# More filler products, a moved gate row, padded w_phi rows and a new nominal order in a fused attention and FFN kernel

## The chip, the cores and the metric

The kernel runs on one core of a Trainium2 chip. The time is the device time of one execution in microseconds (us). The times shown are those of 3 runs of the kernel before; beside them one execution was taken with the hardware profiler, and all rows of the profile come from that one.

## The reference, cut to what matters

The input is one sequence of 2048 tokens with 640 features. Two branches read the same x: a linear attention with 32 heads of 20 features, whose feature map is a softmax of plus and minus a small product with `w_phi`, and a gated FFN with 1728 hidden features. A gate for each token mixes the two.

```python
x = A_x                                                   # 1 x 2048 x 640
g = sigmoid((x * gate_w).sum(-1, keepdims=True))
qkv = (x @ wqkv).reshape(B, S, 3, 32, 20).transpose(2, 0, 3, 1, 4)
pq = einsum("bhsd,hdf->bhsf", q, w_phi)                   # the same for k
phi_q = concat([softmax(pq), softmax(-pq)])               # the same for k
kv = einsum("bhsf,bhsd->bhfd", phi_k, v);  z = phi_k.sum(s)
o = einsum(phi_q, kv) / (einsum(phi_q, z) + 1e-6)
a = o.transpose(...).reshape(B, S, 640) @ wo
b = (gelu(x @ w_gate) * (x @ w_up)) @ w_down              # hidden width 1728
out = g * a + (1 - g) * b
```

## The kernel before, in words

**Tiles.** Tokens are worked in 16 tiles of 128, and for the FFN in 4 blocks of 512. The hidden width is cut into 14 chunks per block (13 of 128 and one of 64 + 64). A chunk is five products for the gate weights `wg` and five for the up weights `wu` (line 647; 128x512 each, over five slices of the 640 features), then a GELU on ScalarE (line 661) and a product on VectorE (line 663). Keys, values and queries of a token tile are two halves of 320 columns, five products each (line 687). Evictions from PSUM go through one helper (line 593 on ScalarE, line 595 on VectorE).

**Folding.** `w_phi` is folded into the key and query weights. It is loaded into `w6`, 120 rows (six heads of 20) by six groups; GpSimd multiplies it with a mask into block-diagonal tiles `BD` (line 606); TensorE multiplies these with the transposed key weights `WkT` (line 621) and the results are evicted into `wK`. The fold has ten steps, for five slices of the features and two halves: groups 0 to 2, and groups 3 to 5. Later the same is done with `WT` for the queries.

**Start-up.** SyncE's queue issues nearly all loads: four token tiles `xtok`, the first 256 columns of `wg` and `wu`, the columns 256 to 640 of both, `w6`, the six transposed loads of `WkT`, the value weights `wV`, and then further FFN weights between transposed loads of x. `w6` takes two loads: one for the groups 0 to 4, one for the 40 rows that the last group has. TensorE first runs 18 useless products on a zeroed tile (`spin`, line 550), then transposes the token tiles 0 and 1 (line 559), runs 5 more useless products, and then the first products with `wg`. The gate vector is loaded as five rows of 128 (`grow`), turned by one tiny transpose on TensorE (line 573), and copied by VectorE (line 575) into a 641st column of `wV`, so that the value product also gives the gate's sums. Its load is issued from ScalarE's queue.

**The order.** The order isn't written by hand. Every operation is entered with a nominal priority, which comes from the table `TIMES` (start of a key group, its period, offsets of exponentials, chunks, folds, queries, attention and down projection) or from numbers beside the call in `startup`. A list scheduler on the host (`schedule`) then plays the program through: it has a duration for each operation, a byte count for each load (all loads share 300 KB per us, and a load counts as landed 1.6 us after its share), five engines and six PSUM banks. At each step it takes the engine that can start something first, and there the ready operation with the smallest priority. `HOLD` makes an operation that needs another ScalarE table look ready that much later. What comes out is the order in which each engine's instructions are emitted; each engine then runs its instructions strictly in that order and waits on semaphores where an operand isn't there.

Dependencies between operations go by cells of 32 bytes of a partition's memory (`CELL`): two operations that touch one cell, one of them writing, are ordered. A row of `w6` before is 20 values of 2 bytes, so 40 bytes a group; the groups 4 and 5 share a cell.

```python
        avail = {e: [] for e in self.obj}
...
            o = min((x for x in lst if from_(x) <= t + 1e-9), key=lambda x: (x.prio, x.idx))
...
            if o.dma:
                dma_free = max(dma_free, t + dur) + o.bytes / 300e3
                o.end = dma_free + 1.6
```

Of the kernel before, what the change touches and what calls it, by code (L numbers as in the profile page):

```python
# [7 lines left out]
P = 128  # L8
# [24 lines left out]
class _Prog:  # L33
# [73 lines left out]
    HOLD = 3.9  # L107
# [163 lines left out]
class _Kernel:  # L271
    S, D, H, F = 2048, 640, 32, 1728
    DH, KD, NT, NB, TB, BT = 20, 5, 16, 4, 4, 512
    NG, HPG = 6, 6
# [14 lines left out]
    def alloc(self):  # L289
# [47 lines left out]
        W = self.HPG * self.DH  # L337
        for name, shape in (("BD", [P, self.NG, W]), ("BM", [P, W]),
                            ("w6", [W, self.NG, self.DH]),
                            ("grow", [KD, P])):  # L340
            setattr(self, name, nc.alloc_sbuf_tensor_at(name, shape, BF, offset=b0))
            b0 += -(-int(np.prod(shape[1:])) * 2 // 64) * 64
# [51 lines left out]
    def at(self, T, fn, *args):  # L394
# [4 lines left out]
    TIMES = dict(wkp=-4.57, dfk=0.51, dfq=0.95, mask=-16.43, fold_k=12.18, t0=33.24, per=21.78, pair=3.13,  # L399
                 exp=3.84, ff=14.55, dff=2.71, fold_q=39.04, rest=-4.17, drest=-3.34, q=-38.61, dq=2.39,  # L400
                 qlate=13.99, q0pre=-21.12, q0exp=-8.41, q0post=1.5, at0=31.81, d0=53.28, q1pre=-18.21,
                 q1exp=2.34, q1post=25.29, f2=28.62, df=1.8, at1=10.48, d1=41.89, q2pre=4.15, q2exp=7.74,
                 q2post=13.74, f3=67.06, at2=21.14, d2=90.12, q3pre=-29.71, q3exp=6.32, q3post=17.94, at3=41.36,
                 d3=45.04)
# [41 lines left out]
    def startup(self):  # L446
        pr = self.pr
        D, KD = self.D, self.KD
        HPG, DH, NG = self.HPG, self.DH, self.NG
# [29 lines left out]
        dma("act", self.grow[:, :], self.gw_d.rearrange("(kt p) -> kt p", p=P), -30.0, 2000)  # L479
# [7 lines left out]
        def ffn_w(i, a, b):  # L487
            n = (b - a) * (1420 if b - a < 512 else 1070)
            dma("sp", self.wg[:, :, a:b], wg_r[:, :, a:b], i, n)
            dma("sp", self.wu[:, :, a:b], wu_r[:, :, a:b], i + 0.01, n)  # L490

        ffn_w(-7.5, 0, 256)
        ffn_w(-4.8, 256, 640)
# [15 lines left out]
        ffn_w(-4.4, 640, 1152)  # L509
# [6 lines left out]
        ffn_w(-4.19, 1152, self.FM)  # L516
# [37 lines left out]
        def tile(t, prio):  # L554
            bk = self.next_a()

            def tr(e):
# [443 lines left out]
```

## Time and profile before

| | |
|---|---|
| median of 3 runs | 293.33 us (291.94 to 294.5) |
| the profiled execution, its own time | 294.05 us |
| its span, first to last instruction | 291.5 us |
| TensorE matmul busy | 285.8 us (98%), 2123 products |
| VectorE busy | 210.7 us (72%) |
| ScalarE busy | 160.8 us (55%) |
| GpSimd busy | 11.6 us (4%) |
| moved by DMA | 24.24 MB, mean 83 GB/s |

The span leaves out what lies around the program, so it is shorter than the execution's own time by 2.55 us. Busy time of TensorE is modelled from the starts of pipelined products, so how fast it runs is read from the distance between starts. In rows of the timeline the columns are start (us), duration (us), engine, line, operation, output and input, shapes, count; in brackets stands the idle time ahead and what ended it. `SPq` is SyncE's queue: there the duration is that of the issue, not of the transfer.

### The profile page before, as it was taken

To read this page: it belongs to the slowest core of one execution; us is meant where nothing else is said; L and a number is where in the kernel's file an instruction comes from. 1 tells how busy PE (TensorE), PEld (TensorE's weight loads), DVE (VectorE), ACT (ScalarE), POOL (GpSimd) and SP (SyncE) were. 2 spreads that over 40 slices of the span, in tenths; PEclk is the share of its full clock that TensorE was granted. 3 is DMA by queue.
4 is the path that set the end of the run, shared out by engine and by line. 5 is a ranking of instruction groups with operands and counts; after the bars stand their busy time and mean duration, and the time that the engine had idled before them with its cause. 6 is when DMAs were issued, how large, how long until landed. Compare 5 with 4: busy or idle time off the path is not lost.

```text
span 291.5 us, 5260 instructions
## 1 busy us (share of the span) xinstructions
PE 285.8 (98%) x2123; PEld 180.8 (62%) x2123; DVE 210.7 (72%) x422; ACT 160.8 (55%) x274; POOL 11.6 (4%) x42
## 2 busy tenths in 40 slices
PE   7999999999999999999999999999999999999996
PEld 6747556567766566456577755655665444777775
DVE  1251799999959999999999999999895332623420
ACT  4318597998686599349917725952861223121121
POOL 8210002100000000000000000000000000000000
PEclk9999999999999999999999999999999999999999
DMA  7969956970000000000455364061313000782421
GB/s 207 199 173 329 176 116 115 297 168 0 2 0 2 0 0 3 0 3 7 92 74 117 93 147 66 9 144 47 72 45 74 0 0 2 135 130 74 92 67 45
DMA packets 61739, 24.24 MB, mean 83 GB/s; under 512 B 52803, under 2 KB 61123, under 8 KB 61715
## 3 DMA queue, kind: packets, MB, share of 16 engines
q1 hardware_dynamic: 60921, 20.83, 33.5%
q0 software_dynamic: 640, 3.03, 3.7%
q8 instruction: 16, 0.26, 0.4%
q14 instruction: 8, 0.07, 0.1%
q10 hardware_dynamic: 154, 0.04, 0.1%
HBM read 8.96 MB, written 2.62 MB: 40 GB/s over the span
## 4 chain that ended last, share of the span: by engine, by line
PE 94%; ACT 2%; DMA 1%; DVE 1%; issue 1%; SPq 0%
PE ps L647 39%; PE ps L687 21%; PE ps L935 21%; PE ps L944 7%; PE ps L756 2%; PE ps L892 2%; DMA wg<-in_B_w_gate_dram 1%; ACT E L803 1%; DVE wK L595 1%; PE ps L621 1%; ACT L803 0%; PE ps L559 0%; SPq L455 0%; ACT Sq L593 0%; ACT gel L661 0%
## 5 line engine op out<-in xcount | busy, mean ns | idle before, releaser
L935 PE MATMUL ps<-wd,hT 128*128 128x320 bf16 (+1 forms) x462 | 65.7, 295 | 0.0
L647 PE MATMUL ps<-xT,wg 128*128 128x512 bf16 (+1 forms) x270 | 63.1, 376 | 0.9 <-DMA wg<-in_B_w_gate_dram 0.8
L647 PE MATMUL ps<-xT,wu 128*128 128x512 bf16 (+1 forms) x270 | 62.7, 374 | 0.0
L661 ACT ACTIVATE gel<-ps 128x512 bf16<-128x512 f32 (+1 forms) x56 | 32.6, 597 | 54.0 <-PE ps L647 53.8
L663 DVE TENSOR_TENSOR hT<-ps,gel 128x512 bf16<-128x512 f32 (+1 forms) x56 | 38.5, 688 | 24.1 <-PE ps L647 23.1
L935 PEld LDWEIGHTS ps<-wd,hT 128*128 128x128 bf16 x462 | 43.5, 98 | 16.2
L821 DVE TENSOR_REDUCE dn<-E 128x132 f32<-128x2640 bf16 x16 | 46.3, 2898 | 4.8 <-ACT E L803 4.7
L950 ACT ACTIVATE osb<-ps,Gm 128x320 bf16<-128x320 f32 (+1 forms) x33 | 16.7, 516 | 52.3 <-PE ps L944 52.1
L647 PEld LDWEIGHTS ps<-xT,wg 128*128 128x128 bf16 x270 | 26.3, 99 | 27.5 <-DVE xT L595 1.4
L647 PEld LDWEIGHTS ps<-xT,wu 128*128 128x128 bf16 x270 | 26.3, 99 | 25.9
L803 ACT ACTIVATE E<-E 128x1320 bf16<-128x1320 bf16 x32 | 40.9, 1307 | 0.6 <-DVE E L796 0.5
L687 PE MATMUL ps<-wK,xT 128*128 128x320 bf16 x160 | 25.7, 299 | 0.7 <-DVE wK L595 0.7
L782 DVE TENSOR_TENSOR t<-t 128x132 bf16<-128x132 bf16 (+1 forms) x96 | 25.2, 262 | 1.0
L687 PE MATMUL ps<-wV,xT 128*128 128x321 bf16 (+1 forms) x160 | 25.7, 300 | 0.0
L687 PE MATMUL ps<-wQ,xT 128*128 128x320 bf16 x160 | 24.4, 299 | 0.2 <-ACT Sq L593 0.2
L687 PEld LDWEIGHTS ps<-wK,xT 128*128 128x128 bf16 x160 | 15.5, 98 | 8.1 <-DVE wK L595 0.8
L900 DVE SCALAR_TENSOR_TENSOR zt<-dn,ps 128x18 f32<-128x18 f32 (+1 forms) x32 | 5.4, 167 | 20.8 <-PE ps L892 20.8
L687 PEld LDWEIGHTS ps<-wQ,xT 128*128 128x128 bf16 x160 | 15.4, 98 | 7.2 <-ACT Sq L593 0.6
L687 PEld LDWEIGHTS ps<-wV,xT 128*128 128x128 bf16 x160 | 15.4, 98 | 7.1
L944 PE MATMUL ps<-wo,OT 128*128 128x320 bf16 (+1 forms) x125 | 19.4, 294 | 0.0
L842 DVE TENSOR_TENSOR E<-E,r 128x2640 bf16<-128x2640 bf16 (+1 forms) x16 | 18.8, 1177 | 0.0
L593 ACT ACTIVATE Sk<-ps 128x320 bf16<-128x320 f32 x32 | 13.9, 448 | 7.2 <-PE ps L687 6.9
(80 smaller groups left out, 254.3 us busy)
## 6 DMA issues: line engine op xcount, KB each, us to landing
out_dram<-osb SPq DMA_DIRECT2D x15, 160.0 KB, 1.8
wd<-in_B_w_down_dram POOLq DMA_DIRECT2D x1, 2080.0 KB, 11.8
wg<-in_B_w_gate_dram SPq DMA_DIRECT2D x2, 640.0 KB, 5.9
wu<-in_B_w_up_dram SPq DMA_DIRECT2D x2, 640.0 KB, 6.6
wV<-in_A_wqkv_dram SPq DMA_DIRECT2D x1, 800.0 KB, 4.7
wo<-in_A_wo_dram POOLq DMA_DIRECT2D x1, 800.0 KB, 12.8
xtok<-in_A_x_dram SPq DMA_DIRECT2D x4, 160.0 KB, 3.3
wg<-in_B_w_gate_dram SPq DMA_DIRECT2D x1, 480.0 KB, 5.7
```

The lines of the kernel that those rows point to most:

```text
L593: self.pr.op("act", lambda e: e.activation(dst, src(), AF.Copy), reads=[bk], writes=[dst], dur=_act(n), prio=prio)
L647: i = e.matmul(out, w[:, kt, :], x[:, kt, :], start=kt == 0, stop=kt == self.KD - 1)
L661: pr.op("act", lambda e: e.activation(g2, self.bank(pg)[r0, :], AF.Gelu_apprx_tanh), reads=[pg], writes=[gs], dur=_act(512), prio=prio, ta ...
L663: pr.op("dve", lambda e: e.tensor_tensor(h, self.bank(pu)[r1, :], g2, ALU.mult), reads=[gs, pu], writes=[h], dur=_dve(512, 1, True), prio= ...
L687: i = e.matmul(self.bank(bk, n), x[:, kt, :], w[:, kt, :], start=kt == 0, stop=kt == self.KD - 1)
L782: pr.op("dve", lambda e: e.tensor_tensor(o, a, b, op), reads=[a, b], writes=[o], dur=_dve(el, rate), prio=T + q)
L803: self.pr.op("act", lambda e, dj=dj: e.activation(dj, dj, AF.Exp), reads=[dj], writes=[dj], dur=_act(1320), prio=T + 0.01 * j, table="exp")
L821: pr.op("dve", lambda e: e.tensor_reduce(dn, d4, AX.X, ALU.add), reads=[d4], writes=[dn], dur=_dve(20 * H), prio=T)
L842: pr.op("dve", lambda e: e.tensor_tensor(dd, dd, m, ALU.mult), reads=[dd, r2], writes=[dd], dur=_dve(20 * H, 2), prio=T + 0.03)
L935: i = e.matmul(out, self.hT[:, hs, c, j * P:(j + 1) * P], self.wd[:, c, c0:c1], start=c == 0, stop=False)
L944: i = e.matmul(out, ot[:, k, :], self.wo[:, k, c0:c1], start=False, stop=k == self.KD - 1)
L950: pr.op("act", lambda e, dst=dst, bk=bk, n=n, gm=gm: e.activation(dst, self.bank(bk, n), AF.Copy, scale=gm), reads=[bk, gm], writes=[dst], ...
```

## The change

Five things are edited together.

- The useless products between the transposes of the token tiles 0 and 1 and the first `wg` products become twelve instead of five.
- The load of the gate row moves from ScalarE's queue to SyncE's, with a priority just behind the four token tiles. The tiny transpose of it gets priority 1.8 instead of 1.4, that is, behind the transposes of the token tiles 2 (1.6) and 3 (1.7).
- `w6` gets rows of 32 values (64 bytes) for each group, of which 20 are used; the loads and the masks address those 20.
- The scheduler's prices of transposed loads change: `WkT` and `WT` 220,000 bytes instead of 400,000 (1.31 us of issue instead of 1.3), x 180,000 instead of 380,000 (1.31 instead of 1.6).
- `HOLD` and the numbers of `TIMES` are replaced, so the order of the whole program is a new one.

The helper `ffn_w` gets more parameters; all calls still use SyncE's queue with the same pieces.

```diff
-    HOLD = 3.9
+    HOLD = 2.7
...
-                            ("w6", [W, self.NG, self.DH]),
+                            ("w6", [W, self.NG, 32]),
...
-    TIMES = dict(wkp=-4.57, dfk=0.51, dfq=0.95, mask=-16.43, fold_k=12.18, t0=33.24, per=21.78, pair=3.13,
-                 exp=3.84, ff=14.55, dff=2.71, fold_q=39.04, rest=-4.17, drest=-3.34, q=-38.61, dq=2.39,
-                 qlate=13.99, q0pre=-21.12, q0exp=-8.41, q0post=1.5, at0=31.81, d0=53.28, q1pre=-18.21,
-                 q1exp=2.34, q1post=25.29, f2=28.62, df=1.8, at1=10.48, d1=41.89, q2pre=4.15, q2exp=7.74,
-                 q2post=13.74, f3=67.06, at2=21.14, d2=90.12, q3pre=-29.71, q3exp=6.32, q3post=17.94, at3=41.36,
-                 d3=45.04)
+    TIMES = dict(wkp=-4.68, dfk=1.33, dfq=1.03, mask=4.05, fold_k=7.07, t0=40.19, per=21.68, pair=1.74,
+                 exp=12.53, ff=13.58, dff=2.78, fold_q=37.53, rest=-3.83, drest=-3.64, q=-38.63, dq=2.6,
+                 qlate=2.49, q0pre=-23.73, q0exp=-9.93, q0post=-1.4, at0=28.67, d0=49.28, q1pre=-19.88,
+                 q1exp=20.95, q1post=23.32, f2=31.46, df=1.8, at1=6.46, d1=40.59, q2pre=5.16, q2exp=9.47,
+                 q2post=16.66, f3=62.88, at2=13.9, d2=88.13, q3pre=-22.09, q3exp=-2.58, q3post=24.93, at3=31.45,
+                 d3=39.23)
...
-        dma("act", self.grow[:, :], self.gw_d.rearrange("(kt p) -> kt p", p=P), -30.0, 2000)
+        dma("sp", self.grow[:, :], self.gw_d.rearrange("(kt p) -> kt p", p=P), -5.9, 2000)
...
-        dma("sp", self.w6[:, 0:NG - 1, :], wphi[0:W * (NG - 1), :].rearrange("(g p) f -> p g f", p=W), -4.75, 240000)
-        dma("sp", self.w6[0:r, NG - 1, :], wphi[W * (NG - 1):, :], -4.74, 20000)
+        dma("sp", self.w6[:, 0:NG - 1, 0:DH], wphi[0:W * (NG - 1), :].rearrange("(g p) f -> p g f", p=W), -4.75, 240000)
+        dma("sp", self.w6[0:r, NG - 1, 0:DH], wphi[W * (NG - 1):, :], -4.74, 20000)
...
-                o = dma("sp", dst[:, g, :], self.wqkv[:, c0:c0 + P], i + 0.001 * g, 400000, transpose=True, dur=1.3)
+                o = dma("sp", dst[:, g, :], self.wqkv[:, c0:c0 + P], i + 0.001 * g, 220000, transpose=True, dur=1.31)
...
-                    -4.3 + 0.1 * b + 0.01 * kt, 380000, transpose=True, dur=1.6)
+                    -4.3 + 0.1 * b + 0.01 * kt, 180000, transpose=True, dur=1.31)
...
-              prio=1.4)
+              prio=1.8)
...
-        spin(5, 1.5, (tile(1, 1.0),))
+        spin(12, 1.5, (tile(1, 1.0),))
...
-            src = self.w6[:, g, :]
+            src = self.w6[:, g, 0:self.DH]
```

More of the change, by code (lines that the diff above doesn't have):

```diff
@@ L485, in startup, with ffn_w @@
         wr = self.wqkv.rearrange("(kt p) n -> p kt n", p=P)
-        def ffn_w(i, a, b):
+        def ffn_w(q, i, a, b, after=()):
             n = (b - a) * (1420 if b - a < 512 else 1070)
[L489 to L493, printed above, removed]
+            dur = 1.0 if q == "pool" else 0.45
+            return dma(q, self.wg[:, :, a:b], wg_r[:, :, a:b], i, n, after, dur=dur), dma(q, self.wu[:, :, a:b], wu_r[:, :, a:b], i + 0.01, n, after, dur=dur)
+        ffn_w("sp", -7.5, 0, 256)
+        p1 = ffn_w("sp", -4.8, 256, 640)
         wphi = self.wphi.rearrange("h d f -> (h d) f")
@@ L508, in startup @@
         dma("sp", self.wP[2][:, :, 0:D], wr[:, :, D2:3 * D], wkp + 0.009, 657000)
-        ffn_w(-4.4, 640, 1152)
+        p2 = ffn_w("sp", -4.4, 640, 1152)
         def x_t(b):
@@ L513, in x_t @@
                 dma("sp", self.xT[:, kt, b * 512:(b + 1) * 512], self.x2[b * 512:(b + 1) * 512, kt * P:(kt + 1) * P],
-                    -4.3 + 0.1 * b + 0.01 * kt, 380000, transpose=True, dur=1.6)
+                    -4.3 + 0.1 * b + 0.01 * kt, 180000, transpose=True, dur=1.31)
         x_t(1)
-        ffn_w(-4.19, 1152, self.FM)
+        ffn_w("sp", -4.19, 1152, self.FM)
         dma("sp", self.wt[:, :, 0:64], wg_r[:, :, self.FM:self.F], -4.18, 81920)
```

## The prediction

> **What bounds the kernel now.** I read the page first, for the share of each engine. Its own time is 294.05 us, its span 291.5 us; the runs shown have a median of 293.33 us, 0.72 us below the profiled one. The sum below is made against 294.05 us and then carried to the median.
>
> ```profile
> span 291.5 us, 5260 instructions
> PE 285.8 (98%) x2123; PEld 180.8 (62%) x2123; DVE 210.7 (72%) x422; ACT 160.8 (55%) x274; POOL 11.6 (4%) x42
> ...
> PE   7999999999999999999999999999999999999996
> ...
> DVE  1251799999959999999999999999895332623420
> ```
>
> TensorE is busy nearly everywhere; only the first slice and the last show idle time. VectorE is full from about 60 us to about 210 us, so it has room before and after, not in the middle. The waits of TensorE, longest first, say how little waiting there is to remove:
>
> ```profile
> PE ps L550 <- DVE gel L464: 1.1, 1, 1.1
> PE ps L647 <- DMA wg<-in_B_w_gate_dram: 0.8, 1, 0.8
> PE ps L687 <- DVE wK L595: 0.7, 1, 0.7
> PE ps L687 <- ACT Sq L593: 0.2, 1, 0.2
> PE ps L647 <- ACT wQ L593: 0.2, 1, 0.2
> ```
>
> A busy TensorE isn't always a fast one, so third I read its timeline over the first 25 us:
>
> ```profile
> 1.06 2.10 PE L550 MATMUL ps<-gel 128*128 128x128 bf16 x18 [1.06 <-DVE gel L464]
> 3.09 0.18 PE L573 MATMUL ps<-ident,grow 5*128 5x5 bf16 x1
> 3.20 1.25 PE L559 MATMUL ps<-ident,xtok 128*128 128x128 bf16 x10
> 4.24 0.74 PE L550 MATMUL ps<-gel 128*128 128x128 bf16 x5
> 5.80 2.29 PE L647 MATMUL ps<-xT,wg 128*128 128x256 bf16 x10 [0.82 <-DMA wg<-in_B_w_gate_dram]
> ...
> 8.42 1.27 PE L647 MATMUL ps<-xT,wu 128*128 128x256 bf16 x5
> ...
> 10.76 1.27 PE L647 MATMUL ps<-xT,wg 128*128 128x256 bf16 x10
> ```
>
> The same ten products of 256 columns take 2.29 us from 5.80 on and 1.27 us from 10.76 on: from start to start 213 ns, then 109 ns. The step comes at about 9.95 us. Before it lie the five filler products and then a hole of 0.82 us. The page's clock row says full speed here; the starts decide. The fourth view is SyncE's queue:
>
> ```profile
> 4.85 0.90 SPq L455 DMA_DIRECT2D w<-in_A_w_phi_dram  x1
> 5.79 11.24 SPq L454 DMA_TRANSPOSE WkT<-in_A_wqkv_dram  x6
> 17.08 0.51 SPq L455 DMA_DIRECT2D w<-in_A_w_phi_dram  x1
> 17.63 0.40 SPq L455 DMA_DIRECT2D wV<-in_A_wqkv_dram  x1
> ```
>
> The six transposed loads of the key weights hold that queue for 11.24 us. By the view of that tile the third is issued at 10.7 and lands 4.7 us later, at 15.4; the sixth is issued at 15.8 and lands at 18.8; wV lands 4.7 us after its issue, at 22.3. These three landings are what the start-up meets next.
>
> **The change part by part.** **(1) Twelve fillers.** Seven more at 107 ns from start to start are 0.75 us, put into 1.03 us of empty time; the first weights land at 5.7 whatever the fillers do, so they cost nothing, and about 0.3 us of hole is left. What they may bring is the clock. Before the step, 15 products at 213 instead of 109 ns lose 1.56 us, and nine transposes at 107 ns against half of it (an estimate from the 256-column ratio) lose 0.48 us: 2.04 us at most. In this trace speed came 4.15 us after the work became unbroken at 5.80; counted from 1.06 the same time ends at 5.2. Bounds: 0 (the hole left still keeps the clock down) and 2.04. I take 1.7, since some first products should still be slow.
>
> [...]
>
> **(2) What is late next.** With 1.7 us gained, the first 512-column product starts at 12.95 - 1.7 = 11.25. Its gate weights land at 3.8 + 5.7 = 9.5, the up weights, wanted at 12.3, at 11.1. Chunks 2 to 4 are 30 products at 216 ns, 6.5 us, and end at 17.7. After them there is only folding, keys and values until the next weights land. Folds of the first half need the third transpose (15.4), of the second half the sixth (18.8), values need wV (22.3). Best case: every fold and key moves up by 1.7. Worst case: the new order asks for them early, since the change prices one transposed load at 220 KB instead of 400 KB. With that price I put the planner's own idea of the third landing near 14.2 and of wV near 18.6, and a value half then stands ahead of the first key half. TensorE would wait there to 22.4, with 0.65 us of second-half folds and 0.68 us of one value half already done: keys start at 23.1, or 21.75 when these 1.33 us are taken off, against 21.06 now, a loss of 0.7 us.
>
> **(3) w_phi in padded rows.** Padded to 64 bytes, the rows of the last group share no 32-byte cell with the first five, so the small second load no longer waits for the big one. It moves from 17.08 up to behind the first, past six transposes, and wV is issued 0.55 us earlier. The six masks on GpSimd, now four at 11.35 and two at 19.03 (0.40 us each), should end at about 13.8. The second-half folds start at 23.1 today, long after both, so that alone brings nothing; it matters only where folds come before 19.9. The larger memset (0.20 us now) ends long before 4.85. Taken together with wV's earlier issue the worst of (2) becomes +0.15, and between -1.7 and +0.15 I take the middle, **-0.8 us** for the start-up.
>
> [...]
>
> **(4) Gate row on SyncE's queue.** One more issue of 0.43 to 0.53 us ahead of the second pair of weights, and with the moved w_phi load about 1.0 us ahead of the key transposes. The first of those now sits 3.5 us in its issue, the later ones 1.27 at least, so 2.2 us of slack covers this; without the cover, up to 1.0 us more. On ScalarE 0.58 us of issue goes ahead of a table load that is wanted only at 3.95: nothing. Its tiny transpose now stands behind tile 3 in priority, at about 8.1; the row lands between its neighbours, 7.7 and 9.5. So 0 to 1.4 us of wait; by the nearer neighbour, 0.
>
> **(5) New nominal order and HOLD 2.7.** Every priority moves. Elsewhere only the 0.7 us on wK (counted above) and 0.4 us on Sq and wQ can be won. ScalarE reloads tables 21 times at 1.28 us and is 45% idle, so a few more loads lie under the products. A bad place can cost several us. I take **+0.5 us**, bounds -0.7 and +4.4 (the slower rival's price).
>
> Sum: -0.8 + 0.5 = -0.3 us, so 293.75 us for a profiled execution like this, and 293.0 us for the median.
>
> **The rivals.** *Full gain.* The clock is up at 5.8 (2.04), the key wait goes (0.7) and the 0.4 us later: -3.1, or 290.2 us. For it: the work behind is all TensorE, back to back, so a gain kept past 22 us is kept to the end. Against it: the three landings, none of which the change moves by more than about half a microsecond.
>
> *VectorE falls behind: the slower side.* The exponentials of a key group get a nominal place 12.53 behind the group's start instead of 3.84, and the reductions follow them. VectorE is idle 9.7 us in 20 to 60 us, and has nothing left later:
>
> ```profile
> 100.00:125.00 25.00, 25.00 (x171) 14.62 (x170) 24.87 (x40) 18.79 (x35) 0.00 (x0) 1.00 0.00 1
> ```
>
> Up to 12.53 - 3.84 = 8.7 us of its early work can slide into the full stretch. The place to pay is 125 to 150 us, where keys end and attention begins and where the chain already runs over exponentials and a table load. If TensorE finds other chunks for half of it, 4.35 us remain: 297.7 us. It decides as soon as the slide is larger than the chunks that are still free to be put in front. Against it: places are only priorities, and an idle engine takes what is ready.
>
> *It doesn't do what it says.* The remaining hole holds the clock down as before; then the start-up stays as it is and only the order counts: 293.33 + 0.5, about 293.8 us.
>
> **How the numbers follow.** Forecast 0.36, full gain 0.26, VectorE behind 0.31, clock unchanged 0.07. About 1% (2.9 us) is what a measurement of this kernel can tell from no change: faster needs 290.4 or less, slower 296.3 or more. Forecast and unchanged clock lie within, so faster 0.26, same 0.43, slower 0.31. The likeliest case alone spans 290.9 to 295.5 (start-up -1.7 to +0.7, order -0.7 to +1.5). With cases on both sides, 289.6 to 298.0 holds the full gain and most of the slow case.
>
> **What would show it.** Right: twelve fillers from about 4.2 to 5.5; the ten first gate products in about 1.1 to 1.5 us; the first 512-column product near 11.3; then waits on WkT or wV between 14 and 23 that eat about half. Wrong on the gain: no such wait, and keys starting near 19.4. Wrong on the clock: 213 ns still at 8 us. Slower: TensorE waiting for VectorE or ScalarE between 110 and 160 us, with VectorE less busy in 20 to 60 us than its 30.3 of 40. The forecast falls if the median lies under 290.9 or over 295.5.

## The result and the profile after

The changed kernel takes **294.21 us** (median of 20 runs, 293.87 to 297.48), beside 293.19 us for 20 runs of the kernel before: a ratio of 1.0052, with a 95% interval of 1.0032 to 1.0073. A second series of the same kernel gave 294.17 us beside 291.96, 1.0070 (1.0045 to 1.0095). So it is slower by half to three quarters of a per cent. The two series differ in the kernel before, whose times fall into two groups (see "The fillers alone, and without"); the changed kernel's median is the same in both. The forecast was 293.0 us and a little faster; the time lies inside the stated range, the sign was wrong.

The profiled execution takes 294.56 us, its span is 292.7 us. The span of the one before was 291.5 us, so spans differ by 1.2 us, and this is the difference that the trace can be asked about. The page's first rows of the changed kernel:

```profile
span 292.7 us, 5291 instructions
PE 285.7 (98%) x2130; PEld 180.0 (61%) x2130; DVE 210.4 (72%) x422; ACT 170.1 (58%) x281; POOL 11.6 (4%) x42
```

TensorE and VectorE are as busy as before. ScalarE has 7 more instructions and is busy for 9.3 us longer (160.8 before). Seven table loads at 1.283 us are 9.0 of it: the page's groups show 14 at line 661 and 13 at line 803 where there were 10 and 9, and one fewer elsewhere, 29 in all instead of 22.

TensorE's waits in the changed kernel:

```profile
PE ps L687 <- DMA wV<-in_A_wqkv_dram: 1.7, 1, 1.7
...
PE ps L621 <- DMA WkT<-in_A_wqkv_dram: 0.6, 1, 0.6
PE ps L687 <- ACT gcol L593: 0.5, 1, 0.5
```

The wait of 0.8 us for the first gate weights and the 0.7 us for wK are gone. In their place stand 1.7 us for wV, 0.6 us for WkT, and 0.5 us for ScalarE. TensorE's timeline of the start-up, cut to the marks that the prediction named:

```profile
4.22 1.49 PE L550 MATMUL ps<-gel 128*128 128x128 bf16 x12
5.94 1.52 PE L647 MATMUL ps<-xT,wg 128*128 128x256 bf16 x10 [0.23 <-issue]
...
11.68 2.32 PE L647 MATMUL ps<-xT,wg 128*128 128x512 bf16 x10
...
18.48 0.56 PE L621 MATMUL ps<-BD,WkT 120*128 120x120 bf16 x9 [0.60 <-DMA WkT<-in_A_wqkv_dram]
...
22.07 1.54 PE L687 MATMUL ps<-wV,xT 128*128 128x320 bf16 x10 [1.66 <-DMA wV<-in_A_wqkv_dram]
23.44 0.29 PE L621 MATMUL ps<-BD,WkT 120*128 120x120 bf16 x3
23.57 2.61 PE L687 MATMUL ps<-wK,xT 128*128 128x320 bf16 x18
```

The ten products behind the fillers take 1.52 instead of 2.29 us, and the first 512-column product starts at 11.68 instead of 12.95: 1.27 us were gained by then. By the start of the keys they are gone. Two value halves stand ahead of the first key half, as the prediction's worst case had it, and TensorE waits for wV until 22.07. The keys start at 23.57 (21.06 before); the two value halves done ahead of them are 10 of the products that came at 23.80 before.

SyncE's queue in the changed kernel shows why these data didn't come earlier:

```profile
3.79 0.38 SPq L455 DMA_DIRECT2D grow<-in_gate_w_dram  x1
...
5.22 2.62 SPq L455 DMA_DIRECT2D w<-in_A_w_phi_dram  x2
7.89 8.62 SPq L454 DMA_TRANSPOSE WkT<-in_A_wqkv_dram  x6
16.55 0.59 SPq L455 DMA_DIRECT2D wV<-in_A_wqkv_dram  x1
```

The gate row and the second w_phi load push the first transposed load from 5.79 to 7.89, but the six are through at 16.5 instead of 17.0. By the view of that tile the third lands at 14.2 (15.4 before) and the sixth at 18.43 (18.76); wV, issued 1.1 us earlier, lands at 22.02 (22.34). The work ahead moved by 1.3 us, the landings that it meets last by 0.3. Even this 0.3 is within what landings vary by: in other traces with this start-up wV lands between 21.5 and 22.6.

To place the whole 1.2 us, I added up for all products how much later than its own length the next one starts (length: 0.417 ns a column, an estimate from this trace, where 512-column products start 215.8 ns apart and 320-column ones 135.8, so 80 ns for 192 columns; it is 213 of the 216 ns between two 512-column products). From before to after this sum changes by -1.40 us in 0 to 10 us, +0.59 in 10 to 20, +0.87 in 20 to 30, +0.69 in 60 to 70, and +0.06 in all the rest. The seven more fillers are 0.37 us of length. So the start-up lost 0.43 us and the stretch at 60 to 70 us lost 0.69; the sum is 1.18. These are losses against an execution of the kernel before whose first products ran at half speed.

The place at 60 to 70 us in the changed kernel, ScalarE's and one TensorE row of the timeline:

```profile
58.70 1.28 ACT L803 ACT_TABLE_LOAD   x1
60.00 1.30 ACT L803 ACTIVATE E<-E 128x1320 bf16<-128x1320 bf16 x1
...
61.52 1.29 ACT L803 ACTIVATE E<-E 128x1320 bf16<-128x1320 bf16 x1
...
63.32 0.18 ACT L593 ACTIVATE gcol<-ps 128x1 f32<-128x1 f32 x1
...
63.49 0.86 PE L687 MATMUL ps<-wV,xT 128*128 128x321 bf16 x5 [0.50 <-ACT gcol L593]
```

ScalarE loads the GELU table at 51.24, the table of the exponentials at 58.70 and the GELU table again at 64.86; from 58.25 to the last of these it has no gap. Evictions queue behind the pair of exponentials, and the value half at 63.49 starts only when the tiny gcol eviction behind them has read its bank. The kernel before has a load ahead of the same pair too, and no such wait; its order gives TensorE another chunk there:

```profile
59.99 1.28 ACT L803 ACT_TABLE_LOAD   x1
...
63.71 1.24 PE L647 MATMUL ps<-xT,wu 128*128 128x512 bf16 x5
```

So it is not a load alone that makes TensorE wait, but a load together with what the order puts behind it.

### The profile page after: what moved, and what is told of

Same layout as the page of the kernel before. It is cut to its first block, busy times and chain, and to the rows that moved or that the text cites. A ratio compares the mean times of both kernels' runs of the same rounds, so it can differ in the third digit from the quotient of the medians.

```text
span 292.7 us, 5291 instructions
## 1 busy us (share of the span) xinstructions
PE 285.7 (98%) x2130; PEld 180.0 (61%) x2130; DVE 210.4 (72%) x422; ACT 170.1 (58%) x281; POOL 11.6 (4%) x42
## 3 DMA queue, kind: packets, MB, share of 16 engines
q1 hardware_dynamic: 60931, 20.84, 34.1%
q0 software_dynamic: 640, 3.03, 3.4%
## 4 chain that ended last, share of the span: by engine, by line
PE 81%; ACT 9%; SPq 4%; issue 2%; DMA 2%; POOL 2%; POOLq 0%
PE ps L647 31%; PE ps L935 21%; PE ps L687 18%; PE ps L944 7%; SPq L454 3%; ACT E L803 3%; PE ps L892 2%; DMA wV<-in_A_wqkv_dram 2%; PE ps L756 1%; ACT L661 1%; ACT L803 1%; ACT gel L661 1%; ACT vaug L593 1%; SPq L455 1%; ACT Sk L593 1%
## 5 line engine op out<-in xcount | busy, mean ns | idle before, releaser
L647 PE MATMUL ps<-xT,wg 128*128 128x512 bf16 (+1 forms) x270 | 62.4, 372 | 0.2 <-issue 0.2
L687 PE MATMUL ps<-wQ,xT 128*128 128x320 bf16 x160 | 25.5, 299 | 0.2 <-ACT gel L661 0.2
L900 DVE SCALAR_TENSOR_TENSOR zt<-dn,ps 128x18 f32<-128x18 f32 (+1 forms) x32 | 5.3, 167 | 22.3 <-PE ps L892 22.1
```

Of the source, the lines that this page charges most:

```text
L647: i = e.matmul(out, w[:, kt, :], x[:, kt, :], start=kt == 0, stop=kt == self.KD - 1)
L687: i = e.matmul(self.bank(bk, n), x[:, kt, :], w[:, kt, :], start=kt == 0, stop=kt == self.KD - 1)
```

## The experiments

My theory behind the result had three parts: (A) the twelve fillers do bring the clock, by which I mean the step from 213 to 109 ns between the starts of 256-column products (the page's clock row shows 9 tenths or more throughout), worth about 1.3 us on the order before; (B) in the new order the gain ends in the waits for WkT and wV; (C) the rest is lost at ScalarE at 62 us, by more table loads and a full queue. The rivals: that the fillers bring nothing, that the new order is slow everywhere, that the gate row's load or the w_phi load did it.

### The fillers alone, and without

In the first, only the number of fillers in the kernel before is changed, and the planner still prices them as five, so its order stays.

```diff
...
-        spin(5, 1.5, (tile(1, 1.0),))
+        spin(12, 1.5, (tile(1, 1.0),), price=5)
```

> The kernel before with twelve fillers instead of five and nothing else: the scheduler is still told the price of five, so every other instruction keeps its place. Theory (the fillers bring the fast clock, and whether that reaches the end is decided by the order behind them): in the order of before, keys come ahead of values and the second-half folds behind three key halves, so no wait on a landing stands in the way; the first 512-column product near 11.3 to 11.7, keys near 19.6 to 19.9 instead of 21.06, and 1.0 to 1.5 us less at the end, ratio 0.995 to 0.997. Rival (the start-up is bound by the landings of the key weights in any order): the chunks start earlier, a wait of the same size appears ahead of the folds or keys, and the ratio is 0.999 to 1.001.

Measured: 0.9970 (0.9946 to 0.9995), 291.88 us beside 292.29, span 290.2 (1.3 less than the profiled execution before). Its timeline:

```profile
6.08 1.60 PE L647 MATMUL ps<-xT,wg 128*128 128x256 bf16 x10 [0.35 <-issue]
...
11.81 2.11 PE L647 MATMUL ps<-xT,wg 128*128 128x512 bf16 x9
...
19.70 2.21 PE L687 MATMUL ps<-wK,xT 128*128 128x320 bf16 x15 [0.67 <-DVE wK L595]
```

The first ten products are through in 1.60 us instead of 2.29. Of the 512-column products the trace lacks the first record (nine where there are ten, and products stand 216 ns apart), so they start at 11.59. That is 1.36 us earlier than before, the keys are 1.36 us earlier too, and nothing takes it back, because here keys come before values and wV isn't missed. The median moves by 0.4 us only. The runs say why: the 12 runs of this kernel lie within 291.27 to 292.42, those of the kernel before in the same series spread over 291.23 to 294.98, a part of them as fast as these.

So I took the five fillers out as well.

```diff
-        spin(5, 1.5, (tile(1, 1.0),))
+        tile(1, 1.0)
```

> The kernel before with none of the five fillers, order otherwise the same. The times of before come in two bunches, near 292 and near 293.5 us. Theory (a longer hole ahead of the first weights makes the late clock the rule): nearly all runs in the upper bunch, median 293.2 to 294.2 us, ratio 1.003 to 1.006, 213 ns at 8 us in the profile. [...]

Measured: 1.0024 (1.0004 to 1.0044), 293.11 us beside 292.26, span 291.4. Ten of 12 runs lie from 292.76 to 293.58, two at 291.7. In its profile the 213 ns between products last to about 9.9 us, and the first ten take as long as in the kernel before:

```profile
5.63 2.29 PE L647 MATMUL ps<-xT,wg 128*128 128x256 bf16 x10 [1.18 <-DMA wg<-in_B_w_gate_dram]
```

The rise is smaller than expected, since the kernel before has many runs of that length itself: of its 133 runs in all series, 72 lie below 292.4 us with most from 291.5 to 292.3, and 61 above with most from 292.8 to 293.8. Twelve fillers leave the lower group, none leaves nearly only the upper one, five give both. How many fall into the upper group differs by series, from 13 of 20 beside the result to 10 of 32, so the median of the kernel before stands at 293.19 in the one and at 291.96 in the other. The profiled execution of before, 294.05 us, was one of the upper group, and so it showed 1.3 us to be won where the median of the series with twelve fillers had 0.4 us to give. No execution of the lower group of the kernel before was traced, so that its clock came early is inferred from the two kernels beside it.

### Five fillers in the changed kernel

```diff
...
-        spin(12, 1.5, (tile(1, 1.0),))
+        spin(5, 1.5, (tile(1, 1.0),), price=12)
```

> The changed kernel with five fillers instead of twelve, the scheduler still told the price of twelve, so every other instruction keeps its place. Theory (in this order the waits for WkT and wV give back all that the clock brings): the first 512-column product about 1.2 us later, the 0.6 us wait on WkT gone, the wait on wV shorter by what remains, the first value half again at 22.0 to 22.2, and the same time as the changed kernel within 0.3 us, ratio to before 1.003 to 1.007. Rival (the clock's gain does reach the end and the loss lies in the later order): 1.0 to 1.5 us longer than the changed kernel, ratio 1.008 to 1.011.

Measured: 1.0071 (1.0045 to 1.0097), 294.58 us, span 292.4. Two rows of its timeline:

```profile
5.82 1.25 PE L647 MATMUL ps<-xT,wg 128*128 128x256 bf16 x10 [1.10 <-DMA wg<-in_B_w_gate_dram]
...
21.66 1.54 PE L687 MATMUL ps<-wV,xT 128*128 128x320 bf16 x10 [1.56 <-DMA wV<-in_A_wqkv_dram]
```

In this execution the products were fast from 5.82 on, right behind a hole of 1.10 us, so the trace alone says nothing on what the fillers do, and the later chunks and the vanished wait for WkT that were expected did not show. The times do: in the new order five fillers cost no more than twelve (1.0071 beside 1.0052 and 1.0070), since the wait for wV ends the start-up either way, here at 21.7 and in the changed kernel at 22.1. Nor do the 12 times fall into two groups 1.5 us apart: ten lie from 294.21 to 295.03. That is (B) from its other side.

### The gate row back on ScalarE

```diff
-        dma("sp", self.grow[:, :], self.gw_d.rearrange("(kt p) -> kt p", p=P), -5.9, 2000)
+        dma("act", self.grow[:, :], self.gw_d.rearrange("(kt p) -> kt p", p=P), -30.0, 2000)
```

> The changed kernel with the gate row's load back on ScalarE's queue; its tiny transpose and copy then come first again on TensorE and VectorE, all else keeps its place. Theory (the gate row's place is worth nothing either way): the gap of 0.15 us around tile 3 goes, the key transposes are issued up to 0.4 us earlier but land within 0.4 us of where they did, ratio to before 1.003 to 1.007, as the changed kernel. Rival (the issue on SyncE's queue delays every landing that the start-up waits for): 0.5 us faster than the changed kernel, ratio 1.003 or less.

Measured: 1.0068 (1.0049 to 1.0087), 294.23 us, the same waits (0.5 us for WkT, 1.5 for wV, 0.5 for gcol). The gate row's move is worth nothing that these times can show.

### The order alone, and all but the order

These two were to split the change: the kernel before with the new `TIMES`, `HOLD` and prices, and the changed kernel with the old ones.

```diff
-    HOLD = 3.9
+    HOLD = 2.7
...
-    TIMES = dict(wkp=-4.57, dfk=0.51, dfq=0.95, mask=-16.43, fold_k=12.18, t0=33.24, per=21.78, pair=3.13,
+    TIMES = dict(wkp=-4.68, dfk=1.33, dfq=1.03, mask=4.05, fold_k=7.07, t0=40.19, per=21.68, pair=1.74,
...
```

> The kernel before with the new TIMES, HOLD and load prices and nothing else: five fillers, gate row on ScalarE's queue, w_phi rows unpadded. With the small w_phi load planned late the scheduler puts the second-half folds and all first key halves ahead of the values. Theory (the loss is the meeting of the new prices with the padded rows, which lets the values slip ahead of the keys, plus a smaller loss later from ScalarE): no wait on wV; a wait of 0.3 to 1.5 us on the last masks or on WkT; about 0.7 us lost at ScalarE later; ratio to before 1.002 to 1.006. Rival (the new order costs the same wherever it stands): ratio 1.007 or more, because the twelve fillers are missing as well.

> The changed kernel with the old TIMES, HOLD and load prices: twelve fillers, gate row on SyncE's queue, padded w_phi rows. In its emitted order key halves stand ahead of the values and the second-half folds behind the first key half. Theory (all of the loss is in the order): as fast as before with twelve fillers alone, keys near 19.7, no wait on WkT or wV over 0.3 us, ratio to before 0.994 to 0.999. Rival (the moved gate row or the padded rows cost something themselves): ratio 1.000 or more, with a wait at the gate row's transpose or later landings of the key weights.

Both expectations were far off. The new order on the old start-up gave 1.0306 (1.0268 to 1.0344), 301.99 us; the old order on the new start-up 1.0335 (1.0298 to 1.0373), 302.81 us. In the second the start-up itself is good, with keys at 19.94; the loss is later, by TensorE's waits:

```profile
PE ps L687 <- ACT Sq L593: 2.8, 2, 2.6
PE ps L647 <- ACT gel L661: 1.3, 1, 1.3
PE ps L647 <- ACT gcol L593: 1.1, 1, 1.1
```

The new order on the old start-up waits 3.9 us for VectorE's O around 156 to 161 us. But the waits aren't all. These are windows of this kernel (behind the window's length stands TensorE's busy time; the third number from the end is its granted clock):

```profile
158.00:160.00 2.00, 0.32 (x5) 0.20 (x5) 2.00 (x8) 0.00 (x0) 0.00 (x0) 0.88 0.00 0
160.00:162.00 2.00, 0.83 (x8) 0.56 (x9) 1.99 (x7) 0.00 (x0) 0.00 (x0) 0.50 0.64 134
162.00:164.00 2.00, 2.00 (x13) 1.21 (x12) 2.00 (x7) 0.53 (x1) 0.00 (x0) 0.50 0.84 182
164.00:166.00 2.00, 1.96 (x17) 1.27 (x16) 1.95 (x9) 1.16 (x2) 0.00 (x0) 0.50 0.71 159
166.00:168.00 2.00, 2.00 (x15) 1.39 (x14) 1.95 (x8) 1.99 (x3) 0.00 (x0) 0.91 0.91 214
```

While TensorE waits here, its granted clock falls from 0.88 to 0.50, and from 162 to 166 us, when the work goes on, it is still 0.50. The five windows lack 3.4 us of full clock, up to 1.1 us of it while TensorE still waited. Its listed waits are 5.8 us longer than in the kernel before and the span is 9.0 us longer, so the waits and the clock make up nearly all of the loss. The old order on the new start-up loses 1.7 us of clock in the same way, from 144 to 150 us behind its wait of 2.6 us, and 7.5 us in waits, where its span is 9.5 us longer; as its start-up is the shorter one, a part stays unexplained there. All 12 runs of the two kernels have a mean granted clock of 0.989 or 0.994.

The nominal numbers are no property of their own: the planner makes a full order out of them together with the operations and prices of the start-up, and a set that fits one start-up gives an order with long waits with another, as far on as 57 to 161 us. The split fails as a split, and the two ratios don't add up to the change's. One thing it does show on the start-up: in both kernels keys stand ahead of values. In the one with the new order they start at 21.92 and values follow at 24.64, with the new prices and the new numbers, but unpadded rows. So the new prices alone did not put the values ahead; it took the padded rows, or another part of the new start-up, as well. No run has the prices alone.

### Keys ahead of values

From here on the planned order is kept and single operations are moved behind others in it, with what depends on them. First the two value halves:

```diff
+        values = [named["half", 2, 0, h] for h in range(2)]
+        order = self.behind(order, values, named["half", 0, 0, 1])
```

> The changed kernel with one move in the emitted order: the first two value halves, with what depends on them, stand behind the first three key halves instead of ahead of them. Nothing else moves. Theory (the first value half waits for wV while keys could run): TensorE waits instead for the last first-half piece of wK, which VectorE finishes at 21.3, so keys start near 21.4 instead of values at 22.07, and the kernel is 0.6 to 0.9 us faster than the changed one, ratio to before 1.001 to 1.004. Rival (the place of the values is not what costs): no change against the changed kernel, ratio 1.004 to 1.007.

Measured: 1.0037 (1.0013 to 1.0061), 293.67 us, 0.9 us below the changed kernel with five fillers in the same series. The wait for wV is gone; the keys start at 21.71, after 0.82 us of waiting for WkT and 0.81 us for the last eviction of wK:

```profile
18.84 0.56 PE L621 MATMUL ps<-BD,WkT 120*128 120x120 bf16 x9 [0.82 <-DMA WkT<-in_A_wqkv_dram]
...
21.71 2.21 PE L687 MATMUL ps<-wK,xT 128*128 128x320 bf16 x15 [0.81 <-DVE wK L595]
```

Part of the loss came back, not all: TensorE now meets the next late thing.

Second, the folds of the second half, which need the sixth transposed load, go behind the last fold of the first half as well:

```diff
+        order = self.behind(order, [named["fold", 1, kt, 1] for kt in range(3)], named["fold", 1, 4, 0])
...
+        order = self.behind(order, [product], evict)     # VectorE's product behind that fold's eviction
         values = [named["half", 2, 0, h] for h in range(2)]
         order = self.behind(order, values, named["half", 0, 0, 1])
```

> The changed kernel with two moves: the values behind three key halves as in the run beside it, and the first three second-half folds behind the last first-half fold, so that nothing waits for the sixth transpose before chunk 4 is done; the eviction of that last first-half fold stands ahead of VectorE's product of chunk 4. Theory (the start-up's waits are all that keeps the clock's gain from the end): no wait on WkT, keys near 19.8 to 20.2, a wait on wV under 0.4 us, and 1.8 to 2.3 us faster than the changed kernel, 0.8 to 1.3 us faster than before, ratio 0.995 to 0.998. Rival (the new order loses its time later, for which the start is no cure): less than 0.8 us gained on the changed kernel, ratio over 1.002.

Measured: 1.0009 (0.9983 to 1.0036), 293.26 us, span 291.6. The timeline of this kernel:

```profile
18.98 0.84 PE L621 MATMUL ps<-BD,WkT 120*128 120x120 bf16 x15
20.65 0.30 PE L621 MATMUL ps<-BD,WkT 120*128 120x120 bf16 x3 [0.83 <-ACT wK L593]
21.03 2.20 PE L687 MATMUL ps<-wK,xT 128*128 128x320 bf16 x15
```

No wait for a load is left, but the last fold of the second half waits 0.83 us for a PSUM bank that an eviction frees. Keys start at 21.03 instead of the expected 19.8 to 20.2, and the gain is 1.3 us, against the changed kernel with five fillers in the same series, where 1.8 to 2.3 were expected. Moving that last fold behind two key halves as well should have won the 0.83:

```diff
-        order = self.behind(order, values, named["half", 0, 0, 1])
+        order = self.behind(order, values, named["half", 0, 1, 0])
+        order = self.behind(order, [named["fold", 1, 4, 1]], named["half", 0, 1, 0])
```

> The changed kernel with folds and keys moved, and a third move: the last second-half fold stands behind two key halves instead of ahead of all, because with the first two moves it waited 0.83 us for ScalarE's evictions; the two value halves come right behind it. Theory (what is left of the start-up's loss is that wait): keys near 20.1 instead of 21.0, no wait over 0.4 us on wV, 0.6 to 0.9 us faster than with folds and keys (1.0009), ratio 0.997 to 0.9995; what still parts it from before with twelve fillers is under 0.7 us and lies at 62 to 70 us. Rival (the wait moves on to the eviction of that fold or to wV): under 0.3 us gained, ratio 1.000 or more.

It did not: 1.0035 (1.0022 to 1.0048), 293.29 us. The keys start at 20.84 behind a wait of 1.21 us for an eviction of wK on ScalarE. In both orders TensorE waits for late evictions.

### An exponential moved at 62 us

```diff
+        acts = [o for o in order if o.eng == "act"]
+        i = acts.index([o for o in acts if o.table == "exp"][5])
+        order = self.behind(order, [acts[i]], acts[i + 3])
```

This is on top of the kernel with folds and keys moved.

> The changed kernel with folds and keys moved as before, and one more move on ScalarE's queue: the second exponential of the pair that runs at 60 to 63 us stands behind the next three evictions instead of ahead of two of them. Theory (the 0.5 us that TensorE waits there for an eviction is due to the exponential ahead of it): that wait goes, nothing new takes its place, and the kernel is 0.4 to 0.7 us faster than with folds and keys alone (1.0009), ratio to before 0.997 to 0.9995. Rival (VectorE is full behind it and a later exponential comes back as a later wait): no gain, ratio 1.000 to 1.002.

Measured: 1.0052 (1.0028 to 1.0075), 294.14 us. The wait before 63.5 us is gone, but the products at 65.5 and 70.1 us are now followed 0.80 and 0.37 us late. Theory and rival both missed: this is 0.9 us slower than folds and keys alone, where at worst no gain was expected. ScalarE's queue is nearly full there (one listed gap, of 0.56 us, from 57.7 to 68.2 us), and this reordering moved the wait and made it longer.

### What table loads cost

First, six more of them in the kernel before, by a tiny exponential ahead of four GELUs of the second block:

```diff
+            if (b, c) in ((1, 7), (1, 9), (1, 10), (1, 11)):
+                e.activation(self.spare[:, c - 7:c - 6], self.bank(pg)[:, 0:1], AF.Exp)
```

> The kernel before with four tiny exponentials put ahead of four GELUs of chunks 7, 9, 10 and 11 of the second token block: six more table loads on ScalarE (7.7 us of its time) between 114 and 130 us, where the changed kernel has most of its seven more. Every other instruction keeps its place. Theory (ScalarE has holes of 2 us there; loads cost only where an eviction that TensorE needs stands behind them): TensorE waits 0 to 0.5 us more, ratio 0.999 to 1.003. Rival (ScalarE's loads are what the later part of the changed kernel loses): 1 us or more, ratio 1.004 or more.

Measured: 1.0142 (1.0093 to 1.0191), 297.35 us beside 292.31. The expected 0.999 to 1.003 was wrong, and the rival's price of over 1 us right. In its list of waits (lines are a few higher in this kernel):

```profile
PE ps L648 <- ACT gel L665: 2.6, 2, 2.1
PE ps L692 <- ACT Sq L594: 1.1, 1, 1.1
```

Six loads are 7.7 us of ScalarE, which is idle for 45% of the span before, and they cost 3.7 us of span (295.2 beside 291.5, both with a late clock), or 5.0 us by the medians. In the 18 us from 113 to 131 us ScalarE was busy 9.48 us before, so there was room for 7.7 in sum; there was none between a gate product and its GELU, which is where the edit puts the loads. In the changed kernel more loads at this time cost nothing that the trace shows: behind 110 us it has 17 loads where there were 13, and the sum of late starts there is 4.04 us beside 4.16.

Then the other way round, loads taken out of the changed kernel:

```diff
...
+        gel = [o for o in order if o.eng == "act" and o.table == "gelu"]
+        for k in (10, 11, 12, 13):
+            gel[k].emit = gel[k].other      # AF.Exp
```

> The changed kernel with the exponential in place of the GELU in the four FFN activations that run between 52 and 67 us (these chunks' values change); every instruction keeps its place, but ScalarE's table loads at 51.2, 58.7, 64.9 and 71.2 us fall away, 5.1 us of its time. Theory (the later loss is ScalarE's loads ahead of evictions that TensorE needs): the wait of 0.5 us on the gate column's eviction at 62 us goes, with nothing in its place, 0.5 to 0.9 us faster than the changed kernel beside it. Rival (the wait comes from the exponentials or from the order itself): the wait stays or moves, under 0.2 us gained.

In the same series the changed kernel ran once more:

> The changed kernel once more, on the same chip as the three runs beside it, so that differences under 1 us can be read. [...] Rival (the waits were that one execution's): waits that differ by over 0.5 us in sum.

Measured: 293.31 us with four loads less, 1.0037 (1.0012 to 1.0063), and 294.17 us for the changed kernel, 1.0070 (1.0045 to 1.0095). The four exponentials take 0.61 or 0.62 us each, the GELUs in their place in the changed kernel 0.60 to 0.65, so only the loads fall away. With them the wait for gcol is gone, that for wV (1.7 us) stays, and 0.86 us are won. Its trace says where: the sum of late starts from 30 to 110 us is 2.14 us, as in the kernel before (2.17), where the changed kernel has 3.03. Of the difference 0.46 us lie at 60 to 70 us, 0.26 ahead of that and 0.17 behind. The profiled execution of the changed kernel run again took 295.03 us, the slowest of its nine. It shows the same waits, 1.8 us for wV, 0.9 for WkT and 0.5 for gcol; by the sum of late starts its start-up lost 1.0 us where the first trace had 0.43. So that term is known to about half a microsecond only. Both cures in one kernel:

> The changed kernel with folds and keys moved and with the four GELUs as exponentials (these chunks' values change). Theory (the two causes are all of the loss and add up): 1.0 to 1.2 us from the start-up and 0.5 to 0.9 from ScalarE, so 1.5 to 2.1 us faster than the changed kernel beside it, and within 0.6 us of the best runs of before. Rival (they overlap, or a third cause is left): under 1.2 us gained.

Measured: 292.09 us, 0.9998 (0.9981 to 1.0016), span 290.3. That is 1.22 us under the kernel with four loads less and 2.08 us under the changed kernel. The two causes add up, and with both removed the changed kernel stands where the kernel before with twelve fillers stands (291.88 us, span 290.2). Against that kernel, whose clock is early as well, the change costs 2.3 us, and the two causes are 2.08 of it.

### The gain without the loss

If the fillers are worth it on the old order, the 0.67 us wait on wK is the longest that is left there. First try: the last fold of the first half goes ahead of chunk 4's up products, three evictions of wK move to ScalarE, and three value halves go behind two more key halves.

```diff
...
+        order = self.behind(order, [pe[i - 1]], pe[i])     # pe[i] is the last fold of the first half
+        order = self.behind(order, [named["half", 2, 0, 0], named["half", 2, 0, 1], named["half", 2, 1, 0]], named["half", 0, 1, 1])
+        for kt in (1, 3, 4):
+            o = [o for o in order if o.eng == "dve" and named["fold", 1, kt, 0] in o.preds][0]
+            o.eng, o.emit = "act", o.other
```

> The kernel before with twelve fillers (order as with five), and three moves in the start-up: the last first-half fold ahead of chunk 4's up products, three of the five first-half evictions of wK on ScalarE instead of VectorE, the first three value halves behind two more key halves. Theory (with the clock up early, the serial evictions of wK are the next thing that is late, then the landing of wV): keys near 19.1 instead of 19.7, no wait on wK over 0.2 us, no wait on wV, and 0.4 to 0.7 us faster than with the fillers alone (0.997), ratio 0.9935 to 0.9965. Rival (ScalarE's evictions are late in turn, or the fold waits for its bank): keys not before 19.5, ratio 0.997 or more.

Measured: 1.0005 (0.9988 to 1.0021), 292.45 us. The keys start at 19.00 without a wait, but the moved value halves had covered the evictions of the second half: the next keys wait 1.36 us for wK at 23.2:

```profile
23.21 1.53 PE L687 MATMUL ps<-wK,xT 128*128 128x320 bf16 x10 [1.36 <-ACT wK L593]
```

The same without moving the values:

```diff
-        order = self.behind(order, [named["half", 2, 0, 0], named["half", 2, 0, 1], named["half", 2, 1, 0]], named["half", 0, 1, 1])
```

> The kernel before with twelve fillers, the last first-half fold ahead of chunk 4's up products, and three of the five first-half evictions of wK on ScalarE; the values stay where they were. Theory (the run before lost 1.36 us because the moved values no longer covered ScalarE's second-half evictions, not because of the rest): keys at 19.0, no wait on ScalarE's wK over 0.3 us, 0.4 to 0.7 us faster than the fillers alone, median 0.8 to 1.5 us under that of before, ratio 0.994 to 0.998. Rival (three evictions on ScalarE cost in any order): a wait of about 1 us behind the key halves again, ratio 0.999 or more.

Measured: 0.9969 (0.9947 to 0.9990), **291.16 us** beside 291.96, span 289.3. The waits of TensorE that are listed for this kernel:

```profile
PE ps L550 <- DVE gel L464: 1.1, 1, 1.1
PE ps L687 <- ACT Sq L593: 0.2, 1, 0.2
PE ps L647 <- ACT wQ L593: 0.2, 1, 0.2
```

The keys start at 18.79, 0.91 us before those of the kernel with twelve fillers alone. Of this 0.30 us were there already at the first 512-column product (11.29 beside 11.59), where the two kernels are alike; so about 0.6 us came from the edit, nearly all of the 0.67. It has the lowest median here and beats both kernels, though by ratio it can't be told from twelve fillers alone (0.9970).

## Why the prediction was right or wrong

- **(1) Twelve fillers: right, a little too large.** 1.7 us were predicted at the first 512-column product, 1.27 came (start at 11.68 instead of 11.3), 1.36 in the kernel before with twelve. But the sum was made against one profiled execution, and what it had to win, a late clock, only part of the runs of the kernel before have. Beside the result 13 of 20 were such runs by their times, so there the comparison held; in the series with twelve fillers the median had 0.4 us to give.
- **(2) What is late next: the step that failed.** It named the place and both ends: wV and WkT as the next late data, and a value half ahead of the keys. Then it took -0.8 us, the middle between -1.7 and +0.15. The runs show the bad end and somewhat more: +0.43 us by the trace (1.0 by a second one), with 1.66 us of waiting for wV and 0.60 for WkT, and 1.22 us that come back when keys and folds go first. There was no reason for a middle: an order is either the one or the other, and the argument at hand spoke for the bad one. With +0.43 in place of -0.8 and the +0.5 of (5) unchanged, the sum would have been +0.9, a slower kernel; the median came out 1.0 above before. What put the values ahead is only in part as argued: by the prediction's estimate the planner has wV at 18.6, and it landed at 22.02, but with the same prices and unpadded rows keys stayed ahead.
- **(3) Padded rows: right on the queue.** The second w_phi load moved up behind the first, wV was issued 1.1 us earlier (0.55 predicted) and landed 0.3 us earlier, and the masks ended at 13.5 (13.8 predicted). Alone it wasn't tried. That the rows may help to let folds and values slip ahead of the keys was not in the prediction.
- **(4) Gate row: right.** Its transpose came at 8.28 (8.1 predicted) without a wait to speak of; moved back, the time is the same.
- **(5) The order: nearly the right sum by a wrong reason.** +0.5 us was taken, the trace shows +0.75 behind 30 us. But a few more table loads were said to lie under the products at no cost. Seven came, net. Behind 110 us that held; before it did not, and four loads taken out between 51 and 72 us give 0.86 us back.
- **VectorE falls behind: wrong.** It had 0.31. VectorE was read as full from 60 us on; its row before is full from 36 us on, with one half-idle slice at 80 to 87, so there was less room to slide into. It is as full as before at 100 to 125 us and as busy in 20 to 60 us (30.2 us), TensorE's one listed wait in 110 to 160 us is 0.2 us for ScalarE, and what grew is ScalarE:

```profile
100.00:125.00 25.00, 25.00 (x173) 15.10 (x172) 24.68 (x48) 24.52 (x42) 0.00 (x0) 1.00 0.00 1
```

In this window of the changed kernel ScalarE is busy 24.52 of 25 us, where it was 18.79. Both kernels have six exponentials there, but six table loads instead of two. Nor did the larger nominal offset move the exponentials back: 26 of the 32 start earlier than before, the first at 36.1 instead of 38.0.

- **Clock unchanged: wrong**, since speed came by about 6.5 us. **Full gain: wrong**, for the reason named against it, the landings.
- **What can be measured.** The prediction held about 1% to be the least change that can be told from none; the interval of the result is 0.2% to either side, so a change of 0.3% can be told.

What stays open: which part of the new start-up, beside the prices, puts the values ahead of the keys, and a part of the 3% that the old order loses on the new start-up.

## What to carry to other kernels

When an edit makes early work faster, read from the queue when the next loads land. Here the work moved by 1.27 us and the landings by 0.3: the gain ended there, and 1.3 us came back with an order that has other ready work in front of the late operand. A planner that is told a load lands earlier than it does (by the estimate, wV at 18.6 instead of 22.02) can put work that needs it ahead of work that could run, and TensorE waited 1.66 us there; correct its prices by landings from the trace and look at the order that comes out, and don't take a middle between two orders. An engine's idle share didn't tell what more instructions cost: six loads of 1.28 us on ScalarE, idle for 45% of the span, made the span 3.7 us longer. Look at whether the load stands between an operand and those who wait for it. And look at more than one execution of the kernel before: here the one that was traced was of the slower of two groups.

## What the runs showed of the hardware

Here a run's time seems to depend on when the clock comes up, that is, when 256-column products start 109 instead of 213 ns apart. The kernel before shows two groups of times, with medians of 291.8 and 293.35 us. Its traced execution, of the upper group, has half-speed products up to about 9.9 us; with twelve fillers speed comes at about 6.8 us, the span is 1.3 us shorter, and no run takes more than 292.42 us. That the clock parts the two groups is inferred from this. Five fillers sometimes bring it early (the changed kernel with five was fast at 5.82 behind a hole of 1.10 us) and sometimes don't (213 ns until 9.95 behind 0.82 us in the kernel before, and until 9.3 and 9.8 in the traces with the order alone and with six more loads).

In the two kernels that split the change, long waits cost TensorE more than themselves: 3.4 us of full clock (up to 1.1 of it during the waits) and 1.7 us are missing there. With the order alone TensorE has waits of 2.53, 1.34 and 0.39 us with little work between them, from 156.6 to 161.7, and then runs at half the granted clock up to about 166.3. The single wait of 1.66 us for wV in the changed kernel did not do this: the products behind it start 146 ns apart once and then 135 to 137 ns, as 320-column products do elsewhere (136). A mean granted clock of 0.994 shows in four more runs, and they are the slowest of their kernels: 297.48 us of the changed kernel, 295.24 with four loads less, 298.06 and 298.86 with six more. None of the four was traced.

A change of table costs ScalarE 1.3 us in this trace: in the changed kernel the load at 58.70 begins 0.02 us or less behind the end of the eviction before it, takes 1.28 us, and the exponential starts at 60.00.
